# The order of the last block's output products, and how its row tiles are stored

## The chip, the cores and the metric

The kernel runs on one core of a Trainium2 chip. The metric is the device time of one execution in microseconds (us), as the median of several runs. A profiled execution gives the span from the first to the last instruction, and the trace of every instruction and DMA packet within it. Engines are named as in the profile: PE is TensorE (PEld its weight loads), DVE VectorE, ACT ScalarE, POOL GpSimd, SP SyncE.

## The reference

Attention over pooled keys and values, then a feed-forward layer with a maximum of three products:

```python
k_p = k.reshape(B, H, Sp, 8, D).mean(axis=3)      # B = H = 8, Sp = 72, D = 64
v_p = v.reshape(B, H, Sp, 8, D).mean(axis=3)
attn = softmax(q @ k_p.T / sqrt(D))
x = (attn @ v_p).transpose(0, 2, 1, 3).reshape(4608, 512)
h = maximum(maximum(x @ w1, x @ w2), x @ w3)      # 512 -> 768
out = h @ w_out                                   # 768 -> 512, float32
```

Only the last line, for the last 512 of the 4608 tokens and for the tile of 128 tokens before them, is touched here.

## The kernel before

The 4608 tokens are worked in nine blocks of 512 (`NB`). The maximum is rewritten as `x w1 + max(0, x (w2-w1), x (w3-w1))`, so that the output of a block is `x wm + hT wo`, where `wm` is the product of `w1` and `w_out`, worked out once, and `hT` holds the hidden values, transposed. Both parts add up in the same PSUM bank.

Blocks up to the eighth go through the generator `project` (L380). It makes one tile of 128 tokens at a time: four matmuls from `xT` and `wm_sb` (L390), a `yield`, six from `hT` and `wo_sb` (L394), a copy from PSUM to the SBUF tile `osb`, and two DMAs to the output (L403), each for 64 of the 128 rows; `u` counts these halves, that is partitions 0 to 63 and 64 to 127. The 64 rows of a half lie nine rows apart in the output, because tokens were regrouped for attention, and each is 2 KB long. Tile 31 (`last`) is the last one of this generator. It is made as two halves of 256 channels, each with its own matmuls, copy (ACT for the first, DVE for the second) and two DMAs, the first on SP, the second on ACT.

The ninth block (`LAST`) has its output from `out_seven` (L637). It splits the tokens in two halves of 256 and the channels in two halves of 256, and makes the four quarters of the output from seven block products in place of eight. `product(i, m)` does product `i` (1 to 7) for sub-tile `m` (0 or 1) of 128 tokens: five matmuls of 128x256 (L669). The operands `so`, `th` and `turns` are the sums and differences made before. Results gather in three kinds of bank per sub-tile:

- bank A takes products 1, 6, 5 and 3, one added to the other. After each, ACT copies the running sum into its quarter of the SBUF tile `ob` (L674);
- bank B takes product 2, which DVE adds to the quarter "first token half, low channels" (L677);
- bank C takes product 7 and then product 4. After 7 (and 5) DVE adds it to "second token half, high channels", after 4 to "first token half, high channels".

`o[:, j, m, :]` is a finished row tile: token half `j`, sub-tile `m`, 128 tokens by 512 channels. `store` sends parts of it out, again as two DMAs for the two sets of 64 partitions.

The order at the end is written by hand (L803 on). After `weave`, which interleaves everything up to the eighth block's hidden values, two more steps of the generator `tiles` end tile 30; then come `fold_h` and the fourteen products in the listed order; then the rest of `tiles`, which is tile 31. Instructions stand on each engine's queue in the order in which the program lists them. In the order before, the low channels of the first token half are stored by POOL after 2b (the letters a and b stand for m = 0 and 1), the second token half as a whole by SP after 3b, and the high channels of the first token half by SP after 4b.

PSUM pools: `PA` has two banks, `BC` and `PO` one each, `SC` two. `project` puts its tiles 29, 30 and 31 into `PO`, `SC` and `PA`.

Of the kernel before, what the change touches and what calls it, by code (L numbers as in the profile page):

```python
# [14 lines left out]
def kernel(  # L15
# [11 lines left out]
    nc = tc.nc  # L27
# [6 lines left out]
    C = H * D  # L34
# [7 lines left out]
    NG = 9  # L42
    GS = (0, 2, 4, 6, 8, 1, 3, 5, 7)
# [3 lines left out]
    TOK = B * S  # L47
# [12 lines left out]
    pools = [first.enter_context(tc.tile_pool(name="ps0", bufs=1, space=PSUM))]  # L60

    def psum(shape, dtype, name, tag, bufs):
        return pools[-1].tile(shape, dtype, name=name, tag=tag, bufs=bufs)
# [59 lines left out]
    for sign in (1, -1):  # L123
        nc.gpsimd.affine_select(
            out=pick, in_=pick, compare_op=ALU.is_ge, fill=0.0, base=7 * (sign < 0),
            pattern=[[sign, 6], [-8 * sign, 128]], channel_multiplier=6 * sign)
    for i in range(3):
        load_w(slice(256 * i, 256 * i + 256))
    nc.gpsimd.dma_start(
        out=wo_sb, in_=moe_w_out.rearrange("(jc p) c -> p jc c", p=128))  # L130
# [140 lines left out]
    SC = ("sc", 2)  # L271
    TR = ("tr", 1)
    PW = ("pw", 3)
# [106 lines left out]
    def project(n):  # L380
        hT = hTs[n]
        for mm in range(4):
            m = 4 * n + mm
            last = m == TOK // 128 - 5
            osb = sb3.tile([128, C], F32, name="osb", tag="osb", bufs=5)
            for c in ((slice(0, C // 2), slice(C // 2, C)) if last else (slice(0, C),)):
                tag = PW if len(pools) < 3 else (PO, SC, PA)[max(0, m - (TOK // 128 - 7))]
                po = psum([128, c.stop - c.start], F32, name="po", tag=tag[0], bufs=tag[1])
                for kc in range(KCH):
                    nc.tensor.matmul(po, xT[:, kc, bass.ts(m, 128)], wm_sb[:, kc, c],  # L390
                                     start=(kc == 0), stop=False)
                yield
                for jc in (0, 3, 1, 4, 2, 5):
                    nc.tensor.matmul(po, hT[:, jc, bass.ts(mm, 128)], wo_sb[:, jc, c],  # L394
                                     start=False, stop=(jc == JCH - 1))
                if c.start:
                    nc.vector.tensor_copy(out=osb[:, c], in_=po)
                else:
                    nc.scalar.copy(out=osb[:, c], in_=po)  # L399
                for u in range(2):  # L400
                    b, g = divmod(2 * m + u, NG)
                    dst = out[S * b:S * b + S, :].rearrange("(r g) c -> r g c", g=NG)
                    (nc.scalar if last and u else nc.sync).dma_start(  # L403
                        out=dst[:, GS[g], c], in_=osb[64 * u:64 * u + 64, c])
            yield


# [89 lines left out]
    def block(n, plan, parts, folds=()):  # L497

        for slot, _ in enumerate(part for stage in parts for part in stage(n)):
# [5 lines left out]
            if folds and slot in FOLDS:  # L505
# [5 lines left out]
              26: [(1, "s0 q2")], 27: [(1, "s1 s2")], 28: [(1, "s3 Q3")],  # L511
              29: [(1, "s4 s5")], 30: [(1, "s6 s7")], 31: [(1, "v0")],
              32: [(1, "v1 x0")], 33: [(1, "X1 v2 v3")]}, (hidden, project))
    load_k(3, nc.gpsimd)
    load_v(3, nc.gpsimd)
# [42 lines left out]
    PA, BC, PO = ("pa", 2), ("bc", 1), ("po", 1)  # L558
# [33 lines left out]
    def turns(n):  # L592
        return (pad3 if n % 2 else pad)[:, 0:4]
# [16 lines left out]
    def out_w(z, r):  # L610

        i, j = divmod(z, 2)
        c = slice(HALF * i, HALF * i + HALF)
        return wm_sb[:, 2 * j + r, c] if r < 2 else wo_sb[:, JH * j + r - 2, c]

    def out_s(z):
        return so["S4"][:, 0:5] if z == 4 else so["S123"][:, 5 * z - 5:5 * z]
# [12 lines left out]
    def fold_h(n):  # L630

        th[n] = ld.tile([128, 4, JH, HALF], F16, name="th", tag="ktFalse")
        h = {i: hTs[n][:, JH * (i // 2):JH * (i // 2) + JH,
                       HALF * (i % 2):HALF * (i % 2) + HALF] for i in range(4)}
        fold_t(nc.vector, h, [th[n][:, i] for i in range(4)])

    def out_seven(n):  # L637

        o = sb2.tile([128, 2304], F32, name="ob", tag="et")[:, 0:2048].rearrange(
            "p (j m c) -> p j m c", j=2, m=2)  # L640
        lo, hi = slice(0, HALF), slice(HALF, C)
        banks, done = {}, set()

        def store(e, j, c):
            for u in range(2):
                b, g = divmod(2 * (4 * n + 2 * j) + u, NG)
                dst = out[S * b:S * b + S, :].rearrange("(r g) c -> r g c", g=NG)
                e.dma_start(out=dst[:, GS[g]:GS[g + 2] + 1:4, c],
                            in_=o[64 * u:64 * u + 64, j, :, c])

        def product(i, m):
            of = "B" if i == 2 else "C" if i in (4, 7) else "A"
            if i in FIRST:
                tag = {"A": PA, "B": SC, "C": BC if m == 0 else SC}[of]
                banks[of, m] = psum([128, 2, HALF], F32, name=f"o{of}", tag=tag[0],
                                    bufs=tag[1])
            p = banks[of, m][:, 0]
            za, zb = PRODUCTS[i]
            for r in range(5):
                c = slice(128 * m, 128 * m + 128)  # L660
                if isinstance(zb, str):
                    z = int(zb[1]) - 1
                    left = turns(n)[:, z, r, c] if r < 2 else th[n][:, z, r - 2, c]
                else:
                    at = HALF * (zb % 2) + 128 * m
                    left = (xT[:, 2 * (zb // 2) + r, NB * n + at:NB * n + at + 128] if r < 2
                            else hTs[n][:, JH * (zb // 2) + r - 2, at:at + 128])
                right = out_s(int(za[1]))[:, r] if isinstance(za, str) else out_w(za, r)
                nc.tensor.matmul(p, left, right, start=(i in FIRST and r == 0), stop=(r == 4),  # L669
                                 skip_group_check=True)  # L670
            done.add((i, m))

            def copy(j, c):
                nc.scalar.copy(out=o[:, j, m, c], in_=p)  # L674

            def plus(j, c, p):
                nc.vector.tensor_tensor(out=o[:, j, m, c], in0=o[:, j, m, c], in1=p,  # L677
                                        op=ALU.add)

            if i in (1, 5, 6, 3):  # L680
                copy(i in (5, 3), lo if i in (1, 3) else hi)
            elif i == 2:
                plus(0, lo, p)
                if m:
                    store(nc.gpsimd, 0, lo)
            elif i == 4:
                plus(0, hi, p)
                if m:
                    store(nc.sync, 0, hi)
            if i in (5, 7) and (12 - i, m) in done:  # L690
                plus(1, hi, banks["C", m][:, 0])
            if i in (5, 7, 3) and all((z, m) in done for z in (5, 7, 3) for m in range(2)):
                store(nc.sync, 1, slice(0, C))

        return product

# [89 lines left out]

    folds = [f for wi in range(1, 3) for f in [fold_w(wi)] * 4]
    block(1, plan1(), (hidden, project))
    for n in range(2, 5):
        block(n, with_keys(n) if n == 5 - 1 else plan(n),  # L790
              (hidden, project))
# [9 lines left out]
    tiles = (t for n in range(5, LAST) for t in project(n))  # L801
# [2 lines left out]
    next(tiles)  # L804
    outs = out_seven(LAST)
    fold_h(LAST)
    for i, m in ((1, 0), (1, 1), (2, 0), (2, 1), (6, 0), (6, 1), (7, 0), (5, 0), (5, 1),
                 (7, 1), (3, 0), (3, 1), (4, 0), (4, 1)):
        outs(i, m)
    for _ in tiles:  # L810
        pass


# [28 lines left out]
```

## Time and profile before

| | |
|---|---|
| time, median of 3 runs | 231.99 us (231.73 to 232.39) |
| the profiled execution | 231.44 us |
| its span | 229.7 us |
| granted PE clock | 0.995 |
| PE busy in the span | 220.6 us |
| last matmul ends | 225.33 us |
| output written after 222 us | about 1 MB, by six DMAs on SP and two on ACT |
| last DMA issued | 226.57 us, on SP |

Times within the trace count from the start of the span. The profiled execution is one run; its 231.44 us stand beside its span of 229.7, and the rest lies before and after the span. A DMA's row on a queue is the time in which the engine issues it; the bytes move later, and the DMA rows and windows show when.

### The profile page before, as it was taken

Reading aid. Unit: us, or ns where it says so; the run is one execution under the profiler, and the core shown is the slowest. Engines: PE = TensorE matmul, PEld = TensorE weight load, DVE = VectorE, ACT = ScalarE, POOL = GpSimd, SP = SyncE. Lnnn points to the kernel's source line nnn. Section 1 sums busy time; section 2 is a strip of 40 time slices with the busy share of each in tenths; the row PEclk is TensorE's granted clock in tenths of the full one; section 3 lists DMA queues with packets and bytes.
Section 4 is the critical chain, followed back from the end, with each engine's and each line's share of the span. In section 5 each row is a group of like instructions: output and inputs, shape, how many; then the busy total and the mean of one; then the engine's idle time right before and its main releaser. Section 6 shows DMA issues by size and latency. Waiting matters only on the chain.

```text
span 229.7 us, 4528 instructions
## 1 busy us (share of the span) xinstructions
PE 220.6 (96%) x1755; PEld 136.4 (59%) x1756; DVE 128.4 (56%) x235; ACT 121.1 (53%) x216; POOL 140.6 (61%) x115
## 2 busy tenths in 40 slices
PE   7788999999999999999999999999999999999992
PEld 2477645568656455545554555455777666786781
DVE  3668875048326333622362246268578887897820
ACT  2277425755864576247524852583776436465330
POOL 7974201999939999999999819920343533920020
PEclk9999999999999999999999999999999999999997
DMA  6999999999559999987998599961430536302326
GB/s 170 209 197 196 211 202 210 195 166 227 98 108 194 219 171 218 193 193 121 211 174 194 102 207 177 172 148 25 94 69 20 130 70 83 91 1 49 82 67 175
DMA packets 47157, 33.53 MB, mean 146 GB/s; under 512 B 27104, under 2 KB 41888, under 8 KB 47136
## 3 DMA queue, kind: packets, MB, share of 16 engines
q0 software_dynamic: 16944, 16.98, 45.8%
q1 hardware_dynamic: 30032, 16.13, 32.8%
q8 instruction: 14, 0.23, 0.4%
q10 hardware_dynamic: 160, 0.13, 0.2%
q14 instruction: 7, 0.06, 0.1%
HBM read 34.60 MB, written 9.44 MB: 192 GB/s over the span
## 4 chain that ended last, share of the span: by engine, by line
PE 89%; DMA 4%; DVE 2%; POOL 1%; issue 1%; ACT 1%; POOLq 0%; DVEq 0%
PE pw L345 27%; PE po L394 18%; PE po L390 12%; PE pA L732 7%; PE psc L206 5%; PE pav L255 4%; DMA vt<-in_v_dram 4%; PE pC L732 3%; PE pm L332 2%; PE oA L669 2%; PE pB L732 2%; PE pxt L245 1%; PE pkt L188 1%; DVE xn L263 1%; PE oC L669 1%
## 5 line engine op out<-in xcount | busy, mean ns | idle before, releaser
L345 PE MATMUL pw<-xT,mw 128*128 128x512 f16 (+1 forms) x336 | 73.1, 349 | 0.3 <-ACT xT L249 0.2
L394 PE MATMUL po<-mwo,hT 128*128 128x512 f16 (+1 forms) x198 | 46.8, 372 | 0.0
L353 DVE TENSOR_TENSOR hT<-t,pw 128x512 f16<-128x512 f16 (+1 forms) x42 | 25.5, 610 | 37.2 <-ACT et L211 25.1
L399 ACT COPY osb<-po 128x512 f32<-128x512 f32 (+1 forms) x32 | 18.5, 578 | 42.2 <-PE po L394 40.2
L345 PEld LDWEIGHTS <-mw 128*128 128x128 f16 x336 | 28.9, 98 | 19.7 <-DVE mw L318 0.6
L211 ACT ACTIVATE et<-psc 72x576 f16<-72x576 f32 (+2 forms) x54 | 35.2, 660 | 6.4 <-PE psc L206 6.2
L150 POOL TENSOR_TENSOR half<-vt 72x2048 f32<-72x2048 f16 x7 | 28.4, 4061 | 13.9 <-DMA vt<-in_v_dram 13.5
L390 PE MATMUL po<-wm,xT 128*128 128x512 f16 (+1 forms) x132 | 33.1, 373 | 0.0
L351 ACT ACTIVATE t<-pw 128x512 f16<-128x512 f32 (+1 forms) x42 | 22.5, 537 | 14.7 <-PE pw L345 13.0
L263 DVE TENSOR_TENSOR xn<-pav,rcp 128x512 f16<-128x512 f32 x40 | 27.7, 692 | 1.4
L394 PEld LDWEIGHTS <-hT 128*128 128x128 f16 x198 | 18.3, 98 | 16.2
L151 POOL TENSOR_TENSOR half<-half 72x1024 f32<-72x1024 f32 (+1 forms) x13 | 27.2, 2095 | 1.0
L206 PEld LDWEIGHTS <-kz 128*128 128x128 bf16 x191 | 17.6, 98 | 14.4 <-ACT qT L183 1.1
L206 PE MATMUL psc<-qT,kz 128*128 128x320 bf16 (+2 forms) x168 | 22.4, 246 | 1.0 <-DVE qT L183 0.9
L150 POOL TENSOR_TENSOR half<-ktFalse 96x1536 f32<-96x1536 f16 x6 | 18.6, 3097 | 5.5 <-DMA ktFalse<-in_k_dram 5.3
L255 PEld LDWEIGHTS <-et 72*128 72x128 f16 x320 | 15.4, 98 | 7.7 <-issue 0.4
L738 ACT CAST pad<-pA 128x512 f16<-128x512 f32 x27 | 15.3, 587 | 8.6 <-PE pA L732 7.2
L261 DVE RECIPROCAL rcp<-pav 128x8 f32<-128x8 f32 x40 | 8.2, 206 | 18.3 <-PE pav L255 18.1
L390 PEld LDWEIGHTS <-xT 128*128 128x128 f16 x132 | 11.9, 98 | 9.0
L255 PE MATMUL pav<-vp,et 72*128 72x65 f16 x320 | 16.9, 194 | 0.1
L713 DVE SCALAR_TENSOR_TENSOR hT<-pad 128x512 f16<-128x512 f16 x18 | 14.6, 819 | 1.8 <-ACT pad L742 1.4
L732 PEld LDWEIGHTS <-sw 128*128 128x128 f16 x144 | 13.7, 98 | 2.8
(106 smaller groups left out, 276.3 us busy)
## 6 DMA issues: line engine op xcount, KB each, us to landing
out_dram<-osb SPq DMA_DIRECT2D x62, 128.0 KB, 2.5
ktFalse<-in_k_dram POOLq DMA_DIRECT2D x7, 576.0 KB, 7.4
qb<-in_q_dram POOLq DMA_DIRECT2D x7, 576.0 KB, 12.7
vt<-in_v_dram POOLq DMA_DIRECT2D x7, 576.0 KB, 11.2
mw<-in_moe_w_dram POOLq DMA_DIRECT2D x9, 256.0 KB, 9.4
ktTrue<-in_k_dram SPq DMA_DIRECT2D x3, 384.0 KB, 5.1
mwo<-in_moe_w_out_dram POOLq DMA_DIRECT2D x1, 768.0 KB, 13.5
qb<-in_q_dram POOLq DMA_DIRECT2D x2, 288.0 KB, 7.8
```

Of the source, the lines that this page charges most:

```text
L150: e.tensor_tensor(out=f, in0=t[:, :, 0:4, :], in1=t[:, :, 4:8, :], op=ALU.add)
L151: e.tensor_tensor(out=f[:, :, 0:2, :], in0=f[:, :, 0:2, :], in1=f[:, :, 2:4, :], op=ALU.add)
L206: nc.tensor.matmul(out, kz_all[b % 2][:, f % 2, h, :], qTs[b][:, n + i0:n + i1, 64 * (h % 2):64 * (h % 2) + 64], start=True, stop=True)
L211: nc.scalar.activation(out=out, in_=in_, func=FT.Exp, scale=1.0 / 64.0)
L255: nc.tensor.matmul(pav[:, h // 4, 65 * (h % 4):65 * (h % 4) + 65], ets[b][:, h, c0:c0 + 128], vp_all[:, b, h, :], start=True, stop=True)
L263: nc.vector.tensor_tensor(out=xn, in0=pv[:, :, :, 0:D], in1=rcp.to_broadcast([128, 2, 4, D]), op=ALU.mult)
L345: mm = nc.tensor.matmul(pw, w_sb[wi][:, kc, bass.ts(jc, 128)], xT[:, kc, col], start=(kc == 0), stop=(kc == KCH - 1))
L351: nc.scalar.activation(out=t, in_=pw, func=FT.Relu)
L353: nc.vector.tensor_tensor(out=hT[:, jc, c0:c1], in0=t, in1=pw, op=ALU.max)
L390: nc.tensor.matmul(po, xT[:, kc, bass.ts(m, 128)], wm_sb[:, kc, c], start=(kc == 0), stop=False)
L394: nc.tensor.matmul(po, hT[:, jc, bass.ts(mm, 128)], wo_sb[:, jc, c], start=False, stop=(jc == JCH - 1))
L732: mm = nc.tensor.matmul(p[:, w], a[:, kc, bass.ts(g, 128)], b[:, kc, :], start=(i in FIRST and w + kc == 0), stop=(w + kc == 2), skip_grou ...
```

## The change

Four things are altered.

1. The order at the end becomes one string. An `F` in it takes one step of tile 31, in four steps: first half from `xT`, first half from `hT` with its copy and stores, second half from `xT`, second half from `hT` with its copy and stores. For that `project` yields once more, after the first half.
2. The products go 1a 1b 2a 2b 6a 7a 6b 5a 7b F 3a 5b F 4a 3b 4b F F, where before they went 1a 1b 2a 2b 6a 6b 7a 5a 5b 7b 3a 3b 4a 4b and tile 31 behind them.
3. `store` sends a whole row tile `o[:, j, m, :]` with rows of 2 KB as soon as its last part is in `ob`: (1,0) after 3a, (0,0) after 4a, (1,1) after 3b, (0,1) after 4b. Partitions 0 to 63 go on SP, 64 to 127 on POOL, or on ACT for (0,1).
4. Tile 31 takes its PSUM from `PO` (one bank) for both halves, not from `PA`.

```diff
@@ project
-                tag = PW if len(pools) < 3 else (PO, SC, PA)[max(0, m - (TOK // 128 - 7))]
+                tag = PW if len(pools) < 3 else (PO, SC, PO)[max(0, m - (TOK // 128 - 7))]
...
+                if last and c.start == 0:
+                    yield
             yield
@@ out_seven
-        def store(e, j, c):
-            for u in range(2):
-                b, g = divmod(2 * (4 * n + 2 * j) + u, NG)
+        def store(j, m):
+            for u, e in enumerate((nc.sync, nc.gpsimd if m < 1 or j else nc.scalar)):
+                b, g = divmod(2 * (4 * n + 2 * j + m) + u, NG)
                 dst = out[S * b:S * b + S, :].rearrange("(r g) c -> r g c", g=NG)
-                e.dma_start(out=dst[:, GS[g]:GS[g + 2] + 1:4, c],
-                            in_=o[64 * u:64 * u + 64, j, :, c])
+                e.dma_start(out=dst[:, GS[g], :], in_=o[64 * u:64 * u + 64, j, m, :])
...
             elif i == 2:
                 plus(0, lo, p)
-                if m:
-                    store(nc.gpsimd, 0, lo)
             elif i == 4:
                 plus(0, hi, p)
-                if m:
-                    store(nc.sync, 0, hi)
+                store(0, m)
             if i in (5, 7) and (12 - i, m) in done:
                 plus(1, hi, banks["C", m][:, 0])
-            if i in (5, 7, 3) and all((z, m) in done for z in (5, 7, 3) for m in range(2)):
-                store(nc.sync, 1, slice(0, C))
+            if i in (5, 7, 3) and all((z, m) in done for z in (5, 7, 3)):
+                store(1, m)
@@ the end
-    for i, m in ((1, 0), (1, 1), (2, 0), (2, 1), (6, 0), (6, 1), (7, 0), (5, 0), (5, 1),
-                 (7, 1), (3, 0), (3, 1), (4, 0), (4, 1)):
-        outs(i, m)
-    for _ in tiles:
-        pass
+    for name in "1a 1b 2a 2b 6a 7a 6b 5a 7b F 3a 5b F 4a 3b 4b F F".split():
+        if name == "F":
+            next(tiles)
+        else:
+            outs(int(name[0]), "ab".index(name[1]))
+    assert next(tiles, None) is None
```

## The prediction

> **What bounds the kernel now.** I read the page's busy shares first, then the chain of waits for the last 15 us, then SP's timeline there, and last the DMA view in short windows. The page says that TensorE does nearly everything:
>
> ```profile
> PE 220.6 (96%) x1755; PEld 136.4 (59%) x1756; DVE 128.4 (56%) x235; ACT 121.1 (53%) x216; POOL 140.6 (61%) x115
> ...
> PE 89%; DMA 4%; DVE 2%; POOL 1%; issue 1%; ACT 1%; POOLq 0%; DVEq 0%
> ```
>
> The chain of waits shows that the part touched here is solid TensorE work, without a gap, until one DVE copy:
>
> ```profile
> 220.95 1.09 PE oA L669 x10
> 222.04 1.09 PE oC L669 x10
> 223.13 0.44 PE po L390 x4
> 223.57 0.66 PE po L394 x6
> 224.22 0.44 PE po L390 x4
> 224.66 0.67 PE po L394 x6
> 225.33 0.03 issue
> 225.35 0.42 DVE osb L397
> ```
>
> So the last result is ready at 225.77, yet the span ends at 229.7. Those 4 us are the tail, and since the change takes no matmul away, only the tail can shrink. SP's timeline (start, duration of the issue) says what fills its first part:
>
> ```profile
> 223.18 1.30 SPq L648 DMA_DIRECT2D out_dram<-ob  x1
> ...
> 224.57 0.60 SPq L648 DMA_DIRECT2D out_dram<-ob  x1
> 225.21 0.61 SPq L648 DMA_DIRECT2D out_dram<-ob  x1
> 225.92 0.56 SPq L403 DMA_DIRECT2D out_dram<-osb  x1
> 226.57 0.66 SPq L403 DMA_DIRECT2D out_dram<-osb  x1
> ```
>
> Four stores of ob and the first half of the last tile stand in front of the store that matters. The last tile's data is ready at 225.77 and goes out at 226.57: 0.8 us of queue. It lands 2.2 us later (228.75), and the closing waits and barrier take the remaining 0.97 us to 229.74. The windows show that the DMA engines are full meanwhile:
>
> ```profile
> 224.00:225.00 1.00, 1.00 (x12) 0.90 (x10) 0.00 (x0) 0.37 (x1) 0.00 (x0) 1.00 0.87 199
> 225.00:226.00 1.00, 0.32 (x3) 0.03 (x1) 0.42 (x1) 0.00 (x0) 0.00 (x0) 1.00 0.93 207
> 226.00:227.00 1.00, 0.00 (x0) 0.00 (x0) 0.00 (x0) 0.00 (x0) 0.00 (x0) 1.00 0.92 260
> 227.00:228.00 1.00, 0.00 (x0) 0.00 (x0) 0.00 (x0) 0.00 (x0) 0.00 (x0) 0.69 0.90 281
> 228.00:229.00 1.00, 0.00 (x0) 0.00 (x0) 0.00 (x0) 0.00 (x0) 0.00 (x0) 0.50 0.18 59
> ```
>
> The last two columns are the DMA share and GB/s: 0.87 to 0.93 for four microseconds. The tail is bound by two things at once, SP's queue and the drain of about 1 MB, whose last packet ends near 228.39. A change must relieve both.
>
> The DMA view gives two more facts:
>
> ```profile
> DMA packets 149, 0.25 MB, mean 192 GB/s; under 512 B 27, under 2 KB 27, under 8 KB 149
> ...
> DMA packets 294, 0.26 MB, mean 350 GB/s; under 512 B 40, under 2 KB 292, under 8 KB 294
> ...
> q8 instruction: 1, 0.02, 5.9%
> ...
> 190.12 1.89 SPq L403 DMA_DIRECT2D out_dram<-osb  x1
> ```
>
> The first line is 217.3 to 218.6, where SP alone stores two 64-partition halves one behind the other. The second is 226.5 to 227.25, where SP's and ACT's stores, of different halves, run together. The third is 223 to 224: one 16 KB packet of instructions, 223.02 to 223.96 in the trace. SP's long issue (1.30 us against about 0.6) lies across it and ends 0.5 us behind it; the 1.89 us issue at 190.12 likewise ends 0.4 us behind such a packet (189.97 to 191.64).
>
> [...] no stretch of this trace has 2 KB stores of both halves together. This is the open cost.
>
> **The change part by part.**
>
> *TensorE order.* The same 14 products (5 matmuls, 0.545 us each) and the two halves of tile 31 (0.44 + 0.66 each) run in another order, so the sum is unchanged if nothing waits. Counting from 2b's end at 217.67, the ends are: 6a 218.22, 7a 218.76, 6b 219.31, 5a 219.85, 7b 220.40, first half of tile 31 begun 220.84, 3a 221.38, 5b 221.93, first half done 222.59, 4a 223.13, 3b 223.68, 4b 224.22, second half 225.33. Products 1, 6, 5, 3 share a bank, so each waits until ACT has copied the one before (0.37). The tightest is 3a at 220.84: 5a's copy ends 220.26, 0.58 to spare. Product 4 needs the DVE add behind 7 (0.42): 4a starts 222.59, add done 220.72; 4b starts 223.68, add done 222.8. The second half, now in the same single bank as the first, starts 224.22; that bank's copy is done 222.99. TensorE: 0, with none of these covers under 0.5 us. If one failed, its whole overrun would go on the path.
>
> *ACT's queue.* The first half's copy ends 222.99 and ACT then issues a DMA (0.50 to 0.56), ahead of 3b's copy, due at 223.71. The cover is 0.15 us; if the issue stalls, store (1,1) waits, but no matmul does. Then ACT issues (0,1)'s second half and the last tile's: nothing else stands behind.
>
> *Stores.* Removed: two POOL stores of 128 KB at 218.5, two of 256 KB and two of 128 KB on SP. Added: four row tiles of 128 KB for SP and 128 KB for POOL (three) or ACT (one). SP issues six either way, but the bytes on SP's ring behind 222 fall from 896 KB (512 + 256 + 128) to 640 KB (4x128 + 2x64). POOL has nothing else to do after 202.5 (it sat idle 16.0 us before its stores); its issues took 0.64 each, landed in 2.3, and hold up nobody.
>
> *Issue times after.* Store (1,0): SP and POOL at 221.9, 0.6 us earlier than before's first. First half of tile 31: ACT and SP at 223.03 to 223.08, just inside the instruction packet, whose place in TensorE's stream I take to be the same. So I let both issues run to about 224.4, as at 223.18 before. SP goes on: (0,0) 224.45, (1,1) 225.05, (0,1) 225.7, last tile 226.3, against 226.57. Without the stall SP would be free at 225.4 and the last store would go at 225.85.
>
> *Drain after, stall included.* First bytes follow an idle queue's issue by 1.12 us (216.14 to 217.26). From 225.5, SP's half of the data is 64 + 3x128 + 64 KB. At 0.66 us per 128 KB (what the second of two stores at 216.14 took) that is 2.64 us with no gap: last packet near 228.05 to 228.1. The other half, on POOL and ACT, starts earlier (POOL's (0,0) at 223.65). Bounds for the two halves together: 350 GB/s, as the mixed stretch shows, makes each half limit itself, and 228.05 stands[...]. I take the first, because the trace measured it here, and keep the other for the range. Receipt 0.36 us (228.39 to 228.75), close 0.97: the last packet moves by 0.34 and the span ends at 229.4.
>
> *Sum.* TensorE 0, ACT 0, tail -0.34. Against the profiled execution: 231.44, of which 229.74 is span and 1.70 lies around it, gives 231.10. The median of the runs is 231.99, 0.55 above the profiled one; I move the median by the same 0.34: **231.65**.
>
> **Rivals.**
>
> *B, no stall (231.2).* The instruction packet falls elsewhere, or the issue slips in before it. Last issue 225.85 in place of 226.57 (-0.72). Drain: (0,0) from 224.8, and 640 KB of both halves plus the last 128 KB at 320 GB/s end by about 227.6 to 227.7, so it no longer decides before the issue. For: the two starts differ by 0.01 to 0.06 us only. Against: all long issues here that lie across such packets waited for their end. -0.75: 231.24.
>
> *C, the drain decides, slower (233.5).* Two queues don't add their halves. Place: DMA engines from 225.4 to the end. Price: 0.92 MB left at that point, because 256 KB that POOL once stored at 218.5 now lie in the tail. It becomes slower than before when the joint rate is under 0.92 MB / 3.0 us = 307 GB/s (with the stall), and slower by 0.3% under about 250[...]. For: 2 KB rows ran at 192 to 207 in every stretch[...]. Against: 350 GB/s in the mixed stretch.
>
> *D, no gain (232.0).* Rate near 305 GB/s, or the end is set by a store on ACT or POOL whose ring waits its turn (ACT's 64 KB at 225.81 landed after 2.6 us against SP's 2.2). 0.
>
> **How the numbers follow.** A 0.46, B 0.24, C 0.15, D 0.15. What a measurement of this kernel can tell is 0.3%, 0.70 us: under 231.29 is faster, over 232.69 slower. A's own range is 231.2 to 232.1. B lies about the bound and gives 0.16 to faster; A's lower edge and wider error give 0.11: faster 0.27. C gives 0.13 to slower and unforeseen stalls 0.03: 0.16. The rest, 0.57, is no change. Range 230.9 to 232.7: it covers A, B and D and leaves out most of C, some 0.15.
>
> **What would show it.** TensorE's last matmul at 225.3 still, without gaps between 215 and 225 (a gap there is a step wrong). An SP or ACT issue of the first half of 1 us or more at 223 (A) or of 0.55 (B). SP's last issue at 226.3 or 225.85. DMA rate over 225 to 228 above 300 GB/s (A, B), or at 200 to 250 with packets past 228.5 (C). Wrong altogether would be a wait of a matmul on ACT behind a stalled DMA issue, or POOL's stores landing last.

## The result, and the profile after

| | before | after | ratio, 95% interval |
|---|---|---|---|
| first comparison (4 runs each) | 232.19 us | 232.08 us | 0.9998 [0.9976, 1.002] |
| second | 231.69 us (35 runs) | 232.32 us (6 runs) | 1.0036 [1.0023, 1.0048] |
| third | 231.76 us (29 runs) | 232.37 us (14 runs) | 1.0027 [1.0013, 1.0041] |

The first comparison shows no change. Its interval is wide enough to hold the forecast too: a gain of 0.34 us is a ratio of 0.9985. The two later ones, which have more runs of the kernel before, show a small loss of about 0.6 us and leave no room for a gain.

The spans of the profiled executions are 229.74 us before and 230.23 us after, but this difference hides a larger one. In the changed kernel's profile the product 1a, which stands before everything that was changed, already starts 0.40 us sooner (214.93 against 215.33). So from here on the measure is the **tail**: from the end of the last DVE copy (line 397) to the end of the span. Where a time is called "behind" or "ahead of" the copy, or has a minus sign, it counts from the end of that copy. Before, the copy ends at 225.78 and the tail is 3.96 us. After, it ends at 225.38 and the tail is 4.85 us, 0.89 us longer. Two more profiles of the changed kernel gave 4.82 and 4.89 us.

The chain of waits of the changed kernel, its end (start, duration, piece):

```profile
222.73 0.55 PE oA L670 x5
223.28 0.55 PE oC L670 x5
223.83 0.44 PE po L390 x4
224.26 0.67 PE po L394 x6
224.93 0.02 issue
224.95 0.42 DVE osb L397
```

It is as solid as before: from the start of 1a to the end of the last matmul it takes 10.00 us in both profiles, so TensorE lost nothing by the new order. What follows the copy is on SP and ACT. Their DMA issues in the timeline after (start, duration):

```profile
222.62 0.47 SPq L403 DMA_DIRECT2D out_dram<-osb  x1
222.63 0.56 ACTq L403 DMA_DIRECT2D out_dram<-osb  x1
223.22 0.51 SPq L650 DMA_DIRECT2D out_dram<-ob  x1
223.82 1.76 SPq L650 DMA_DIRECT2D out_dram<-ob  x1
224.32 1.26 ACTq L650 DMA_DIRECT2D out_dram<-ob  x1
225.68 0.82 SPq L650 DMA_DIRECT2D out_dram<-ob  x1
...
226.60 0.56 SPq L403 DMA_DIRECT2D out_dram<-osb  x1
```

Two stores, (1,1) on SP and the second half of (0,1) on ACT, take 1.76 and 1.26 us and both end at 225.58. SP's store (0,1) has to wait for that, and the last store of tile 31 goes out 1.22 us behind the copy. Before, it was 0.79 us. POOL's two stores, issued in the same microsecond, show nothing of the kind:

```profile
223.49 1.07 POOL L650 DMA_DIRECT2D out_dram<-ob  x2 [1.21 <-DVE ob L678]
```

The DMA view of 223.6 to 225.2 holds a packet of instructions, and the windows after give DMA share and GB/s in the last two columns:

```profile
q8 instruction: 1, 0.02, 6.1%
```

```profile
223.00:224.00 1.00, 1.00 (x12) 0.89 (x10) 0.33 (x2) 0.37 (x1) 0.52 (x1) 1.00 0.78 221
224.00:225.00 1.00, 0.92 (x9) 0.58 (x6) 0.33 (x2) 0.00 (x0) 0.55 (x2) 1.00 0.86 203
225.00:226.00 1.00, 0.00 (x0) 0.00 (x0) 0.38 (x1) 0.00 (x0) 0.00 (x0) 1.00 0.69 228
226.00:227.00 1.00, 0.00 (x0) 0.00 (x0) 0.00 (x0) 0.00 (x0) 0.00 (x0) 1.00 0.82 220
227.00:228.00 1.00, 0.00 (x0) 0.00 (x0) 0.00 (x0) 0.00 (x0) 0.00 (x0) 1.00 0.83 273
228.00:229.00 1.00, 0.00 (x0) 0.00 (x0) 0.00 (x0) 0.00 (x0) 0.00 (x0) 0.54 0.36 94
```

The packet is 16 KB and runs from 223.62 to 225.19 in the trace. It took 1.56 us, against 0.94 before, where the DMA engines were idle for most of it. The long issues end 0.39 us behind it. The windows show the second thing: although the stores now stand on two or three queues, the engines move 203 to 228 GB/s over 223 to 227. Before, they moved 199 and 207 over 224 to 226 and then already 260.

### The profile page after: what moved, and what is told of

Same layout as the page of the kernel before. It is cut to its first block, busy times and chain, and to the rows that moved or that the text cites. A ratio compares the mean times of both kernels' runs of the same rounds, so it can differ in the third digit from the quotient of the medians.

```text
span 230.2 us, 4534 instructions
## 1 busy us (share of the span) xinstructions
PE 221.1 (96%) x1756; PEld 136.6 (59%) x1756; DVE 127.7 (55%) x235; ACT 121.3 (53%) x216; POOL 140.9 (61%) x116
## 4 chain that ended last, share of the span: by engine, by line
PE 89%; DMA 4%; DVE 2%; POOL 1%; issue 1%; ACT 1%; POOLq 0%; DVEq 0%
PE pw L345 27%; PE po L394 18%; PE po L390 12%; PE pA L730 7%; PE psc L206 5%; PE pav L255 4%; DMA vt<-in_v_dram 4%; PE pC L730 3%; PE pm L332 2%; PE oA L670 2%; PE pB L730 2%; PE pxt L245 1%; PE pkt L188 1%; DVE xn L263 1%; PE oC L670 1%
```

## The experiments

Three theories were set against each other. The first: issues on SP and ACT stand still behind such a packet of instructions. The second: the bytes of the tail and the rate at which they leave decide. The third: the order makes row tiles late. All tails are of one profiled execution, all ratios are against the kernel before on the same chip. One tail alone is weak evidence: two profiles of one kernel, stores_early, differ by 0.51 us.

| kernel | tail, us | ratio, 95% interval |
|---|---|---|
| before | 3.96 | 1 |
| after (again, third) | 4.85 (4.82, 4.89) | 1.0036 [1.0023, 1.0048], 1.0027 [1.0013, 1.0041] |
| a_shift: after, packet moved | 4.34 | 1.0018 [1.0008, 1.0027] |
| b_shift: before, packet moved | 3.66 | 1.0005 [0.9986, 1.0023] |
| order_only | 5.57 | 1.0061 [1.0049, 1.0073] |
| stores_only | 3.84 | 0.999 [0.9975, 1.0005] |
| early_lo: after, with the early POOL store | 3.73 | 1.0005 [0.9991, 1.002] |
| stores_early: order of before, early POOL store, row tiles on two queues | 3.17 (3.68) | 0.997 [0.9956, 0.9983], 0.9962 [0.9952, 0.9972] |
| stores_early_shift | 3.22 | 0.9974 [0.9961, 0.9987] |
| early_one_queue: stores_early, all on SP | 6.27 | 1.0077 [1.0058, 1.0095] |

**The changed kernel again.** No edit.

> The changed kernel once more. Tail means the time from the end of the last DVE copy (line 397) to the end of the span: 3.96 us in the profile before, 4.85 us in the first profile after. Theory 1 (issues on SP and ACT stand still behind a packet of PE instructions): again an SP or ACT store issue of 1.2 us or more that ends 0.3 to 0.5 us behind the 16 KB packet, tail 4.2 to 4.9 us, time within 0.3% of before. Theory 2 (the DMA engines' joint rate decides): no tie of the long issues to the packet, rate under 250 GB/s over the whole of 225 to 228, same tail. If the first profile was an accident, the tail falls to about 3.3 us and the time by 0.6 us.

The tail was 4.82 us. SP's store (1,1) took 1.73 us and ACT's 1.22 us, both begun under a packet of 1.61 us; the time was 1.0036 of before. So the first profile was no accident.

> The changed kernel a third time, for its time alone: the first comparison gave a ratio of 0.9998, the second 1.0036. With a tail 0.9 us longer than before in two profiles, 1.002 to 1.004 and a tail of 4.8 us.

Tail 4.89 us, SP's issue 1.65 us, ratio 1.0027. ACT's issue was short this time (0.48 us), though it too began under the packet.

**The packet moved.** The page of the profile counts 14 such packets on q8, beside about 3,500 matmul and weight-load instructions, and does not say whose instructions they hold. That they are TensorE's was the author's estimate. If so, 102 more of its instructions at the start, at equal work, move the packet of the tail to an earlier time:

```diff
-        for _ in range(n):
-            nc.tensor.matmul(wm, warm[:, 0:128], warm, start=True, stop=True)
+        for _ in range(4 * n):
+            nc.tensor.matmul(wm[:, 0:128], warm[:, 0:128], warm[:, 0:128], start=True, stop=True)
```

> The changed kernel with the 17 warm-up matmuls of 512 columns at the start cut into 68 of 128 columns: the same PE time, 102 PE instructions more, so that the packet of PE instructions of the tail comes about 5.6 us earlier, before any store. Theory 1: no issue over 0.8 us on SP or ACT in the tail, the last SP store issued within 0.2 us of the DVE copy's end, tail 3.0 to 3.5 us, time 0.6 to 1.2 us under the changed kernel's. Theory 2: the tail stays at 4 us or more although no issue is long.

The packet came 7.81 us ahead of the copy's end, in place of 1.75, and the issues in the tail became short. SP's stores (1,1) and (0,1) and both last stores of tile 31, from the timeline of a_shift:

```profile
224.29 0.55 SPq L650 DMA_DIRECT2D out_dram<-ob  x1
...
224.93 0.55 SPq L650 DMA_DIRECT2D out_dram<-ob  x1
...
225.88 0.47 SPq L403 DMA_DIRECT2D out_dram<-osb  x1
225.88 0.50 ACTq L403 DMA_DIRECT2D out_dram<-osb  x1
```

The last stores go out 0.03 us behind the copy, 1.2 us sooner than in the changed kernel. So the stall is tied to the packet. More than issues comes late with it: POOL's half of (1,0), issued 3.7 us ahead of the copy in both kernels, took 4.5 us from its issue to its landing where the packet followed, and 2.7 us in a_shift. The tail fell by 0.51 us, to 4.34, and is still above that of the kernel before. The time, 1.0018, is not clearly apart from the changed kernel's, since the intervals overlap. So the first theory is right about the issues, but the stall is only a part of what was lost. The windows of a_shift:

```profile
223.00:224.00 1.00, 1.00 (x11) 0.90 (x10) 0.42 (x1) 0.28 (x2) 0.05 (x1) 1.00 0.82 217
224.00:225.00 1.00, 1.00 (x11) 0.89 (x10) 0.42 (x1) 0.16 (x1) 1.00 (x2) 1.00 0.73 209
225.00:226.00 1.00, 0.39 (x4) 0.10 (x1) 0.42 (x1) 0.00 (x0) 0.01 (x1) 1.00 0.98 287
226.00:227.00 1.00, 0.00 (x0) 0.00 (x0) 0.00 (x0) 0.00 (x0) 0.00 (x0) 1.00 0.94 275
227.00:228.00 1.00, 0.00 (x0) 0.00 (x0) 0.00 (x0) 0.00 (x0) 0.00 (x0) 1.00 0.92 313
```

Now the DMA engines are busy to the end, at 0.92 to 0.98: this tail is a drain of bytes. From 225 on they move 275 to 313 GB/s, where the stalled kernel moved 220 to 273. Even so the first two microseconds run at 209 to 217 GB/s. The packets in the trace suggest why. For store (1,0), SP's half moves from -2.84 to -2.05 (us from the copy's end) and POOL's from -2.22 to -1.31. POOL's issue came 0.28 us behind SP's and its first byte 1.46 us behind its issue, against 1.12 on SP. So the two halves of this store follow each other more than they run together. That this alone keeps the rate low was not tested.

> The same shift in the kernel before. Theory 1: SP's second store of the second token half takes 0.65 us in place of 1.30, so the last store goes 0.65 us sooner, unless the drain of the single queue holds it; tail 3.3 to 3.9 us. Theory 2: the tail stays at 3.9 to 4.0 us, because the bytes set it.

SP's second store took 0.62 us in place of 1.30, the last one went out at 0.47 in place of 0.79, and the tail was 3.66. One other issue took 0.87 us. The ratio can't be told from 1. So the kernel before had lost about 0.3 us of tail to its own packet. With both packets out of the way the changed kernel's tail is still about 0.7 us longer (4.34 against 3.66), so of the 0.89 us between the two kernels the stall explains about 0.2.

**The parts of the change.** order_only keeps the new order and takes the old `store` and its three calls back; stores_only keeps the new `store` and its calls and takes the old list of products back.

> The changed order of products and of tile 31's halves, with the stores of the kernel before (POOL after 2b, SP's two large ones after 3b, SP's two others after 4b). SP still has four ob stores ready only at 3b and 4b, and the first half of tile 31 in front of them. Theory 1: one of these issues lies across the instruction packet, tail 3.9 to 4.6 us. Theory 2: the bytes of 2 KB rows come out at 190 GB/s from one queue at a time, tail 4.2 us or more. Both: PE ends without gaps, so the order alone costs PE nothing.

5.57 us, 1.0061: beyond the first theory's figure, and far over the bound of 4.2 us that the second gave. No issue in it is longer than 0.85 us, although SP's at -1.66 (0.65 us) began under the packet (-2.02 to -0.92); so not every issue under a packet is held. The time went elsewhere. SP's stores of `ob` start only when 3b is done. That is 1.66 us before the copy's end, in place of 3.30, because tile 31's first half and 4a now lie ahead of 3b. The windows of order_only, whose copy ends at 225.75, show the engines half idle before it and full long after it:

```profile
224.00:225.00 1.00, 1.00 (x11) 0.89 (x10) 0.42 (x1) 0.06 (x1) 0.00 (x0) 1.00 0.52 125
225.00:226.00 1.00, 0.29 (x3) 0.01 (x1) 0.42 (x1) 0.00 (x0) 0.00 (x0) 1.00 0.60 135
226.00:227.00 1.00, 0.00 (x0) 0.00 (x0) 0.00 (x0) 0.00 (x0) 0.00 (x0) 1.00 0.96 207
227.00:228.00 1.00, 0.00 (x0) 0.00 (x0) 0.00 (x0) 0.00 (x0) 0.00 (x0) 1.00 0.93 277
228.00:229.00 1.00, 0.00 (x0) 0.00 (x0) 0.00 (x0) 0.00 (x0) 0.00 (x0) 0.72 0.89 284
```

> The changed stores (each row tile whole, on two queues) with the order of the kernel before: all products first, tile 31 behind them. The row tiles are then ready about 1.1 us earlier than in the changed kernel. Theory 1 (issues behind the instruction packet): the packet comes 2.75 us before the last copy's end, an SP or ACT store issued then takes 1.2 us or more; the last SP issue is still late, tail 3.7 to 4.3 us. Theory 2 (bytes in the tail): 256 KB that went out early on POOL are late now, but all row tiles start 1.1 us sooner than in the changed kernel, so tail 3.6 to 4.1 us, under the changed kernel's 4.8. Theory 3 (the order itself costs, by delaying row tiles): time 0.5 us or more under the changed kernel's.

3.84 us and 0.999. The profiled execution was the slowest of its 14 (232.90 us, median 231.45), so the ratio is the better witness. SP's store (0,0) took 1.10 us across the packet, and the last SP issue came at 0.34. The tail of 3.84 us lies within the figures of the first and the second theory; the time, some 0.4% under the changed kernel's, is what the third asked for. The tail is 1.0 us shorter than the changed kernel's, and the only edit between them is the order. With the products all ahead of tile 31, SP issues (1,1) 1.7 us, (0,0) 0.5 us and (0,1) 1.8 us sooner against the copy; (1,0) goes out 0.1 us later. But the packet too lies elsewhere: it ends 1.95 us ahead of the copy in place of 0.19. Against a_shift, which has no stall in the tail, stores_only is 0.5 us shorter. So the order is worth 0.5 to 1.0 us of tail, if a stall can only lengthen it.

**The bytes that had gone out early.** The kernel before sends 256 KB, the low channels of the first token half, 7 us before the copy's end. early_lo puts that back into the changed kernel:

```diff
             elif i == 2:
                 plus(0, lo, p)
+                if m:
+                    early()
...
+        def early():
+            for u in range(2):
...
+                nc.gpsimd.dma_start(out=dst[:, GS[g]:GS[g + 2] + 1:4, lo],
+                                    in_=o[64 * u:64 * u + 64, 0, :, lo])
...
-                store(0, m)
+                store(0, m, hi)
```

> The changed kernel, but the low channels of the first token half go out on POOL after 2b as in the kernel before, and the stores after 4a and 4b carry the high channels alone. Theory 2: 256 KB less in the tail, last packet 0.8 to 1.0 us sooner, tail 3.8 to 4.1 us, time back to that of the kernel before. Theory 1: as many issues in the same places, the stall stays and with it the last SP issue at 1.2 us behind the copy; tail 4.3 us or more.

```profile
225.00:226.00 1.00, 0.16 (x2) 0.00 (x0) 0.42 (x1) 0.00 (x0) 0.00 (x0) 1.00 0.69 176
226.00:227.00 1.00, 0.00 (x0) 0.00 (x0) 0.00 (x0) 0.00 (x0) 0.00 (x0) 1.00 0.92 280
227.00:228.00 1.00, 0.00 (x0) 0.00 (x0) 0.00 (x0) 0.00 (x0) 0.00 (x0) 1.00 0.44 120
```

The last packet ends at 2.27 in place of 3.45, the tail is 3.73 and the time that of the kernel before. So the bytes count, as the second theory says, but the 1.1 us of tail are not theirs alone. The stall was there and shorter: SP's (1,1) took 1.11 us under a packet of 0.98 us, and the last SP issue came at 0.30 in place of 1.22. Against a_shift, which has no stall in the tail, early_lo is 0.6 us shorter. The early bytes are thus worth 0.6 to 1.1 us of tail, again if a stall can only lengthen it. early_lo with the packet moved, which would decide, was not run.

**All together.** stores_early takes the order of before, keeps that early store, and sends the rest as row tiles on two queues.

> The order of the kernel before, the early POOL store kept, and the other three quarters in row tiles on two queues. Theory 2: the bytes of the tail as before (1 MB) but in both partition halves at once and 0.5 us sooner in bytes; tail 3.3 to 3.7 us, time 0.3 to 0.6 us under the kernel before. Theory 1: the issue of (0,0) on SP and of (0,1) on ACT stand across the packet until about 1.0 us before the copy's end; the rest follows in time, the last SP issue within 0.4 us of the copy.

The last stores, in the timeline of stores_early, whose copy ends at 225.74:

```profile
225.77 0.47 ACTq L403 DMA_DIRECT2D out_dram<-osb  x1
...
225.94 0.55 SPq L403 DMA_DIRECT2D out_dram<-osb  x1
```

and its windows:

```profile
223.00:224.00 1.00, 1.00 (x11) 0.90 (x10) 0.43 (x2) 0.00 (x0) 0.76 (x2) 1.00 0.84 217
224.00:225.00 1.00, 1.00 (x11) 0.89 (x10) 0.00 (x0) 0.37 (x1) 0.00 (x0) 1.00 0.97 307
225.00:226.00 1.00, 0.28 (x3) 0.00 (x0) 0.42 (x1) 0.00 (x0) 0.00 (x0) 1.00 0.69 224
226.00:227.00 1.00, 0.00 (x0) 0.00 (x0) 0.00 (x0) 0.00 (x0) 0.00 (x0) 1.00 0.70 190
227.00:228.00 1.00, 0.00 (x0) 0.00 (x0) 0.00 (x0) 0.00 (x0) 0.00 (x0) 1.00 0.49 119
```

SP's issue across the packet is there (1.13 us) and costs nearly nothing, because it is over 1.5 us before the copy. The engines reach 307 GB/s before the copy and are no longer full after it (0.49 to 0.70). Tail 3.17 us, time 230.96 against 231.65 us. This version beats the kernel before.

> stores_early once more, beside the changed kernel on the same chip: tail 3.2 us, ratio 0.996 to 0.998, 1.4 to 1.7 us under the changed kernel.

0.9962, 1.5 us under the changed kernel's 232.37 on the same chip, so it beats both kernels. The tail was 3.68, though: the packet came at -1.80 here and at -2.88 in the first profile of the same kernel. SP and ACT took 0.68 and 0.66 us for tile 31's first half, begun under it, stores landed 4.1 us after their issue in the median, and SP's last issue waited 0.7 us for an earlier store of `ob` to land.

> The same with the instruction packet moved 5.6 us ahead (68 short warm-up matmuls for 17 long ones). Theories 1 and 2 together: no long issue, last issues at the copy's end, DMA engines idle before it, tail 2.9 to 3.3 us, time 0.6 to 1.0 us under the kernel before. If neither names the bound, the tail stays above 3.6 us.

3.22 us and 0.9974: against the first profile of stores_early (3.17 us, 0.997) moving the packet adds nothing. With the stores early enough, a stall of SP has room.

**One queue in place of two.**

```diff
-            for u, e in enumerate((nc.sync, nc.gpsimd if m < 1 or j else nc.scalar)):
+            for u, e in enumerate((nc.sync, nc.sync)):
```

> stores_early with both partition halves of the row tiles on SP, one behind the other. If the second queue is what helps (both halves of the partitions in flight, and fewer issues on SP), SP has eight ob issues of 0.5 us or more, one of them across the instruction packet, and the tail goes back to 3.9 to 4.6 us, time at or over that of the kernel before. If sending row tiles early is enough, the tail stays at 3.2 to 3.4 us.

6.27 us and 1.0077, far beyond the figure expected. The last issues of SP, and the windows from 227 on:

```profile
227.32 0.59 SPq L655 DMA_DIRECT2D out_dram<-ob  x1
228.00 0.55 SPq L403 DMA_DIRECT2D out_dram<-osb  x1
228.64 0.55 SPq L403 DMA_DIRECT2D out_dram<-osb  x1
```

```profile
227.00:228.00 1.00, 0.00 (x0) 0.00 (x0) 0.00 (x0) 0.00 (x0) 0.00 (x0) 1.00 0.52 136
228.00:229.00 1.00, 0.00 (x0) 0.00 (x0) 0.00 (x0) 0.00 (x0) 0.00 (x0) 1.00 0.48 121
229.00:230.00 1.00, 0.00 (x0) 0.00 (x0) 0.00 (x0) 0.00 (x0) 0.00 (x0) 1.00 0.38 92
```

The last one goes out 3.03 us behind the copy. Ten issues of about 0.6 us and one stall of 1 us are more than SP has time for. The engines move 92 to 136 GB/s from 227 on and are half idle, so this tail is bound by issues, not by bytes. Row tiles on one queue lose 2.3 us of tail against the kernel before, which has four stores of `ob` on SP where this one has eight; only the second queue makes row tiles a gain.

## Why the prediction was right or wrong

The time lies in the range, and no change was the likeliest class. But that was luck in so far as the tail, the only term that was forecast to move, became 0.89 us longer and not 0.34 us shorter. The range was wide enough for the loss of about 0.6 us that the second and third comparison show. So the reasons need sorting.

- **TensorE's order at 0: right.** The chain has no gap, and every cover held. The tightest, 0.58 us in front of 3a, was not used up.
- **The stall behind the instruction packet: right in kind, wrong in place and size.** It was put on tile 31's first half, with the packet from 2.75 us before the copy's end and 0.94 us long. In the three profiles after it came 1.75, 1.91 and 1.73 us before it and took 1.44 to 1.61 us. So tile 31's first half went out in 0.47 and 0.56 us, and (1,1) and (0,1) were held. The last SP issue was to come 0.53 us behind the copy; it came at 1.22. Worth 0.5 us of tail by a_shift. Rival B, no stall, is answered by the same run: it expected 0.75 us less than before, and the tail was 0.38 us longer.
- **The drain: this step failed.** It read "350 GB/s, as the mixed stretch shows, makes each half limit itself, and 228.05 stands", that is a last packet 2.28 us behind the copy. (The sum behind that figure is slightly off: 225.5 plus 2.64 is 228.14, a gain of 0.25 us and not 0.34.) It came at 3.45. The tail moved 203 to 228 GB/s over 223 to 227. Up to 225 the rate is as low without the stall (209 and 217 in a_shift), where the halves of the store looked at hardly overlapped. From 225 to 227 it goes with the stall: a_shift moved 287 and 275 there. The 350 GB/s came from a stretch in which SP's queue was already backed up and rows were 1 KB. As a rate it is not far off: a_shift reached 313 and stores_early 307 GB/s over a whole microsecond, of 2 KB rows and others. It was taken for a stretch in which the queues were not yet backed up and an issue stood still.
- **The receipt**, the time from the last packet's end to the landing of the last store, was taken as 0.36 us, and was 0.47 (3.45 to 3.92).
- **The early 256 KB** were named only in rival C, as its price. They were worth 0.6 to 1.1 us of tail, and 0.2 to 0.3% of time by early_lo against the changed kernel. So C was right about its price, and about a low rate for the first two microseconds. Its ground, that two queues don't add their halves, does not hold for later ones (313 and 307 GB/s). Its figure of 233.5 was too high: it was the author's estimate, with the engines at about 200 GB/s to the end, and they moved 220 to 273 from 225 on.
- **Not priced at all: the new order makes the row tiles late.** With tile 31's first half among the products, and 4a ahead of 3b, 3b moves 1.6 and 4b 1.1 us toward the end. The prediction counted this on TensorE, as 0, and let the stores follow from it, but never asked what the new stores would do with the old order: stores_only is 0.5 to 1.0 us of tail shorter.

So a true gain and two losses lie in the change. Row tiles on two queues, with the rest as before, gain: stores_early is 0.3 to 0.8 us of tail and 0.3 to 0.4% of time under the kernel before. Giving up the early store takes back 0.2 to 0.7 us of tail in the order of before (3.84 against 3.68 and 3.17) and 0.6 to 1.1 us in the new one. The new order takes back 0.5 to 1.0 us. These don't add exactly, since the stall falls on another issue in each.

What stays open: how the packet of instructions and the long issues on SP and ACT hang together, and when an issue becomes long. That they are tied is shown by moving the packet: SP's store (1,1) took 1.76 us in the changed kernel and 0.55 in a_shift. The same is seen earlier in the changed kernel's trace: SP's issues at 127.32, 176.17 and 189.81 took 1.07, 1.21 and 1.48 us and each ended 0.4 us behind such a packet. But several issues under a packet took no longer than others (0.65 us in order_only, 0.48 in after_third, 0.55 and 0.56 on ACT in stores_only and stores_early), and what makes the difference was not tried. Nor was it settled what sets its place. With the new order it came 1.73 to 2.02 us ahead of the copy in all five profiles that did not move it; with the old one 2.71 to 2.88 us in four and 1.80 us in one. Open, too, is why the first comparison shows nothing where two later ones show 0.3%; its interval, up to 1.002, overlaps only the third's.

## What to carry to other kernels

In the last microseconds, list for each store when its data is ready, when its queue is free, and how many bytes are still to go behind it: bytes that can leave early should, even if a single larger store looks tidier (here 256 KB, worth 0.6 to 1.1 us of tail). An order that finishes outputs one by one loses if it brings the bulk of them closer to the end (here 0.5 to 1.0 us). A rate read off one stretch may not hold where the queues are less full or an issue stands still (350 GB/s was read off, 203 to 228 came over 223 to 227).

## What the runs showed of the hardware

- Output stores on SP and ACT whose issue begins while a 16 KB packet of instructions moves on q8 often have a long issue, which in the traces of before and after ends 0.3 to 0.5 us behind that packet. In the last microseconds SP's took 1.76 (after), 1.73 (after_again), 1.65 (after_third), 1.30 (before), 1.13 (stores_early), 1.11 (early_lo) and 1.10 us (stores_only), against 0.5 to 0.6 for others. POOL's two stores issued beside the packet of after took 0.55 and 0.53 us.
- A store issued before the packet can land late: POOL's half of (1,0) took 4.5 us from issue to landing in the changed kernel, 2.7 us in a_shift.
- The packet of the tail took 0.94 us with the DMA engines mostly idle (before) and up to 1.61 us among stores (after_again).
- 102 more short matmul and weight-load instructions at the start, with the same matmul work, moved it from 1.75 (after) to 7.81 us (a_shift) before the copy's end.
- With stores of both partition halves in flight the engines moved 307 (stores_early, 224 to 225) and 313 GB/s (a_shift, 227 to 228) over a microsecond, with one half after another 192 (before, 217.3 to 218.6).
